# Runs of four chunks of V, eight score pairs between them, and one head's scores in a dense bank

## The chip, the cores and the metric

The kernel runs on one core of one Trainium2 chip. The metric is the device time of one execution in microseconds; before the change its median over three runs is 1396.16 us (1395.28 to 1396.99).

## The reference

One transformer block: layer norm, attention with 32 query heads of 16 dimensions and one shared key and value head, a residual, a second layer norm and a GEGLU feed-forward, all in float32 for 2048 tokens of 512 features.

```python
def _A_ref(x, wq, wk, wv, wo):
    q = (x @ wq).reshape(B, S, H, Dh)       # B, S, D, H = 1, 2048, 512, 32; heads ahead of tokens
    k = x @ wk
    v = x @ wv
    scores = jnp.einsum("bhqd,bkd->bhqk", q, k) * (Dh ** -0.5)
    p = _softmax(scores, axis=-1)
    o = jnp.einsum("bhqk,bkd->bhqd", p, v)
    return o.transpose(0, 2, 1, 3).reshape(B, S, H * Dh) @ wo
...
def _B_ref(x, w_gate, w_up, w_down):        # w_gate, w_up: 512 x 1792
    return (_gelu(x @ w_gate) * (x @ w_up)) @ w_down
...
h = x + _A_ref(_layernorm(x, axis=-1), A_wq, A_wk, A_wv, A_wo)
h2 = h + _B_ref(_layernorm(h, axis=-1), B_w_gate, B_w_up, B_w_down)
```

## The kernel before

The queries are taken in four blocks of 512 tokens (b). Attention goes through a block by eight groups of four heads (g), and through each group by sixteen chunks of 128 keys (kc), so there are 512 chunks in all. For a chunk, TensorE makes two **score pairs** (`scores`, L363). A pair is two heads that run side by side in the two row halves of the array, the contraction rows 0 to 63 and 64 to 127, and fills one buffer `s` of two PSUM banks. ScalarE turns each pair into weights with one exponential of 1024 columns (L374), which goes to half of the tile `p`. The chunk's **V matmuls** (`weigh`, L376) then multiply the four heads' weights by V, in four column tiles of 32, into `acc`. The profile counts each of these float32 matmuls twice, so a chunk is eight rows there. There are two `s` buffers, five `p` buffers (`PB`) and one `acc`.

The **dense work** of a block, its output projection (`pp`), gate, up and down products (`pg`, `pu`, `pd`), is done while attention goes through the next block. Each product is a sum of 9 to 18 terms with a contraction of 128. It is computed in two halves: `rows(0)` runs all terms with the contraction rows 0 to 63, `rows(1)` with rows 64 to 127, each into a bank of its own, and VectorE adds the two. A call of `step` (L837) issues one half step of each, the second one `LAG` = 6 steps behind, and the two run side by side in the array as the heads of a score pair do. Three PSUM banks (`spare`, d0 to d2) go round among the halves; a bank goes to the end of the list when its last matmul is issued, and whoever takes it next waits until it was read.

The order on TensorE, ScalarE and GpSimd is the one in which the code is written, and in the loop at L1167 that holds for SyncE and VectorE too. The loop goes through `CYCLES`. A woven cycle first finishes two or three pending chunks (`finish`, the V matmuls; `evacuate` after a group's last chunk) and then follows a string in which `s` is a score pair and `d` a dense step. Three cycles, with 3, 3 and 2 chunks, are one list: 8 chunks, 16 score pairs and 36 dense steps. Where too few steps are available, the second string is used, with a chunk (`v`) after every second pair and no dense work: a **pause**. Ahead of a cycle, `before` issues the tanh of finished gates (`bend`), the work that is left for VectorE (`later`), and the transpositions of the second layer norm's output (`turn`, L621), which take one of the three dense banks.

In the last block nothing is left to weave, and its dense work is the tail (`last_dense`) after the loop.

Of the kernel before, what the change touches and what calls it, by code (L numbers as in the profile page):

```python
# [9 lines left out]
F32 = mybir.dt.float32  # L10
# [9 lines left out]
P = 128  # L20
# [32 lines left out]
BOUND_LISTS = (3, 4)  # L53

HOLD = -4

# [3 lines left out]
def kernel(  # L60
# [97 lines left out]
    def run(outer, first):  # L158
# [204 lines left out]
        def scores(i, p, qg, kc, u):  # L363

            third = width == 1 and (2 * i + u) % 3 == 2
            pool, tag, bufs = (ps, "s3", 1) if third else (pss, "s", 2)
            s = pool.tile([P, 2, T], F32, tag=tag, bufs=bufs, name=f"s_{i}_{u}")
            for a in range(2):
                rows = slice(64 * a, 64 * a + KR)
                nc.tensor.matmul(  # L370
                    s[:, a, :], kaug[rows, kc * P : (kc + 1) * P], qg[rows, u, :],
                    start=True, stop=True,
                )
            nc.scalar.activation(p[:, 2 * u : 2 * u + 2, :], s, AF.Exp, scale=SCALE)  # L374

        def weigh(acc, p, kc):  # L376
            for j in range(4):
# [428 lines left out]
        built = []  # L806

        def rows(a):
            nonlocal at
            i = 0  # L810
            while i < len(queue):
                name, n, terms, done, ready = queue[i]
                i += 1
                if a == 0:
                    assert ready is None or ready()
                    left[0], at = n, i
                    built.append([])
                    source = iter(terms())
                sent = built[i - 1]
                tag, bank = take_bank(f"{name}_{a}")  # L820
                r = slice(64 * a, 64 * a + 64)
                for k in range(n):
                    if a == 0:
                        sent.append(next(source))
                        left[0] -= 1
                    lhsT, rhs, _ = sent[k]
                    nc.tensor.matmul(  # L827
                        bank, lhsT[r], rhs[r], start=(k == 0), stop=(k == n - 1),
                        skip_group_check=True,
                    )  # L830
                    if k == n - 1:
                        spare.append(tag)
                        done(a, bank)
                        side(2)
                    yield

        def step(first=True):  # L837
# [4 lines left out]
            if ahead > LAG or not first:  # L842
                assert ahead > 0
                next(seconds)
                ahead -= 1

# [197 lines left out]

        cur = {}

        def score(n):

            nonlocal acc
            i, u = divmod(n, 2)  # L1050
            b, r = divmod(i, PER)
            g, kc = divmod(r, KC)
            if u == 0:
                if kc == 0:
                    cur["qg"] = qgs.pop((b, g))
                    acc = psa.tile([P, T], F32, tag="acc", bufs=1, name=f"acc_{b}_{g}")
                if kc == 2 and b * NG + g + 1 < NB * NG:
                    key = divmod(b * NG + g + 1, NG)
                    qgs[key] = load_q(*key)
                cur["p"] = sb.tile([P, 4, T], F32, tag="p", bufs=PB, name=f"p_{i}")  # L1060
            scores(i, cur["p"], cur["qg"], kc, u)
# [11 lines left out]
        width = 1  # L1073


        n, lead = 0, 2 * PER + 23
        with tc.manual_schedule(engines={mybir.EngineType.SP, mybir.EngineType.DVE}):
            parts = None
            if first:
                work = later_q()  # L1080
                parts = part_weights(early.enter_context(tc.tile_pool(name="parts", bufs=1)))


            normed = True
# [12 lines left out]
            def norm():  # L1097
                nonlocal normed
                if not normed:
                    next(work)  # L1100
                    normed = True

            def pace():
                nonlocal n, parts, db, tiny
                if n == 2 * PER:
                    drain()
                    for _ in parts or ():
                        pass
# [12 lines left out]
                if n == 2 * PER + 8:  # L1121
                    prime()

            moves = {"s": pace, "p": visit, "n": norm, "v": partial(finish, 1)}
            for move in OPENING + PERIOD * (PER // KC):
                moves[move]()
            while n < lead:
                pace()
                if n % 4 == 2 and len(pend) > 2 and n < lead - 1:
                    finish(1)  # L1130
                elif n % 4 == 0:
                    finish(len(pend) - 2)
# [5 lines left out]
        def catch_up():  # L1138
            while ahead > 0:
                step(False)  # L1140
# [23 lines left out]
        fixed.enter_context(  # L1164
            tc.manual_schedule(engines={mybir.EngineType.SP, mybir.EngineType.DVE})
        )
        for i in range(-((lead - end) // 16)):  # L1167
            if first and i in BOUND_LISTS:
                bound_flag(BOUND_LISTS.index(i))
            for count, woven, plain in CYCLES:  # L1170
                idle = available() < woven.count("d")
                if idle:
                    while available():
                        step()
                    if at == len(queue) or queue[at][0].startswith("pg"):
                        catch_up()
                bent = before(idle)
                if n == end and not last_x:
                    prepare_x()
                if not idle:  # L1180
                    finish(count)
                for key in bent:
                    later.extend(gate(*key))
                for move in plain if idle else woven:
                    if move == "d":
                        step()
                    elif move == "v":
                        if n == end and not last_x:
                            prepare_x()
                        finish(1)  # L1190
                        clock += 4
                    elif n < end:
                        score(n)
                        n += 1
                        clock += 1
# [386 lines left out]
```

## Time and profile before

| what | value |
|---|---|
| median of three runs | 1396.16 us |
| the profiled execution: its own time / its span | 1397.61 us / 1395.8 us |
| granted TensorE clock | 1.000 |
| ScalarE's share of the span / VectorE's | 74% / 47% |
| loop with the woven dense work, about 304.8 to 1252.6 us | 947.8 us |
| tail after it | 143.2 us |
| number of V runs in the whole program, of 3, 2 and 1 chunks | 91, 86, 67 |

PE is TensorE, PEld its loads of weights, ACT ScalarE, DVE VectorE. A row of the timeline has the start, the length, the engine, the line of the program, what is written from what, the shape and, behind it, how long the engine sat idle before it and on whom it waited. Rows of one kind that follow each other are merged: the length is then that of all. The length of one matmul covers its way through the array, and matmuls overlap, so the distance between starts tells what one costs.

### The profile page before, as it was taken

Reading aid. Unit: us, or ns where it says so; the run is one execution under the profiler, and the core shown is the slowest. Engines: PE = TensorE matmul, PEld = TensorE weight load, DVE = VectorE, ACT = ScalarE, POOL = GpSimd, SP = SyncE. Lnnn points to the kernel's source line nnn. Section 1 sums busy time; section 2 is a strip of 40 time slices with the busy share of each in tenths; the row PEclk is TensorE's granted clock in tenths of the full one; section 3 lists DMA queues with packets and bytes.
Section 4 is the critical chain, followed back from the end, with each engine's and each line's share of the span. In section 5 each row is a group of like instructions: output and inputs, shape, how many; then the busy total and the mean of one; then the engine's idle time right before and its main releaser. Section 6 shows DMA issues by size and latency. Waiting matters only on the chain.

```text
span 1395.8 us, 25287 instructions
## 1 busy us (share of the span) xinstructions
PE 1379.5 (99%) x10406; PEld 753.3 (54%) x10406; DVE 651.0 (47%) x1097; ACT 1034.1 (74%) x1157; POOL 239.8 (17%) x346
## 2 busy tenths in 40 slices
PE   9999999999999999999999999999999999999998
PEld 7533333325555555545555555545555555558886
DVE  7413131314354444548364444448364453546665
ACT  8799999997787777877787777787778777772000
POOL 7576777621000000002000000001000000011000
PEclk9999999999999999999999999999999999999999
DMA  5565776753232333311522433321433333233552
GB/s 163 167 216 184 235 235 233 220 181 133 73 106 74 118 104 103 116 60 46 181 94 81 134 103 103 104 66 31 148 103 104 118 103 103 91 123 126 187 205 94
DMA packets 66783, 180.32 MB, mean 129 GB/s; under 512 B 9672, under 2 KB 9672, under 8 KB 66628
## 3 DMA queue, kind: packets, MB, share of 16 engines
q1 hardware_dynamic: 55324, 143.29, 31.0%
q0 software_dynamic: 10208, 35.26, 7.6%
q8 instruction: 84, 1.38, 0.4%
q14 instruction: 39, 0.32, 0.1%
q10 hardware_dynamic: 1128, 0.07, 0.1%
HBM read 130.87 MB, written 47.45 MB: 128 GB/s over the span
## 4 chain that ended last, share of the span: by engine, by line
PE 94%; ACT 2%; DMA 1%; DVE 1%; issue 1%; SPq 0%; POOL 0%; ACTq 0%; POOLq 0%
PE acc L378 33%; PE s L370 20%; PE pg L827 9%; PE pu L827 8%; PE pd L827 7%; PE pq L219 3%; PE pd L865 3%; PE pg L865 3%; PE pu L865 3%; PE pp L827 2%; ACT p L374 2%; PE pp L929 1%; PE pd_rest L877 1%; DMA x<-in_A_x_dram 1%; PE pk L1327 1%
## 5 line engine op out<-in xcount | busy, mean ns | idle before, releaser
L374 ACT ACTIVATE p<-s 128x1024 f32<-128x1024 f32 x1024 | 959.6, 1037 | 223.7 <-PE s L370 220.6
L378 PE MATMUL acc<-p,v_sb 128*32 128x512 f32 x4096 | 490.0, 598 | 0.0
L370 PE MATMUL s<-qg,kaug 50*128 50x512 f32 x1984 | 388.3, 426 | 4.2 <-ACT p L374 4.1
L370 PEld LDWEIGHTS s<-qg,kaug 50*128 50x128 f32 x1984 | 169.4, 184 | 281.7 <-ACT p L374 123.5
L378 PEld LDWEIGHTS acc<-p,v_sb 128*32 128x32 f32 x4096 | 108.7, 109 | 233.1 <-issue 218.7
L827 PE MATMUL pg<-x2h,w 64*128 64x512 f32 x672 | 175.2, 392 | 0.0
L827 PE MATMUL pu<-x2h,w 64*128 64x512 f32 x672 | 174.5, 392 | 0.0
L827 PE MATMUL pd<-w,gh 64*128 64x512 f32 x624 | 124.7, 394 | 1.9 <-DVE h L615 1.6
L757 DVE TENSOR_TENSOR h<-h,pd 128x512 f32<-128x512 f32 x80 | 55.0, 687 | 140.7 <-PE pd L827 140.6
L137 POOL TENSOR_SCALAR rstd<-mv 128x1 f32<-128x1 f32 x16 | 3.6, 223 | 649.1 <-DVE mv L135 648.8
L827 PEld LDWEIGHTS pg<-x2h,w 64*128 64x128 f32 x672 | 95.5, 186 | 11.4
L827 PEld LDWEIGHTS pu<-x2h,w 64*128 64x128 f32 x672 | 95.7, 186 | 10.8
L827 PE MATMUL pg<-x2l,w 64*128 64x512 f32 x336 | 99.9, 392 | 0.0
L827 PE MATMUL pu<-x2l,w 64*128 64x512 f32 x336 | 99.9, 391 | 0.0
L827 PEld LDWEIGHTS pd<-w,gh 64*128 64x128 f32 x624 | 69.7, 185 | 15.0 <-DVE h L615 2.5
L391 DVE COPY oT<-acc 128x512 f32<-128x512 f32 x32 | 22.1, 692 | 112.5 <-PE acc L378 112.3
L983 ACT ACTIVATE ga<-ga 128x512 f32<-128x512 f32 x14 | 8.8, 632 | 88.5 <-DVE ga L980 88.5
L827 PE MATMUL pd<-w,gl 64*128 64x512 f32 x312 | 72.1, 392 | 0.0
L694 DVE TENSOR_TENSOR g<-g,pg 128x512 f32<-128x512 f32 x42 | 28.8, 685 | 90.8 <-PE pg L827 90.8
L414 DVE RECIPROCAL oc<-oc 128x128 f32<-128x128 f32 x64 | 56.7, 923 | 21.4 <-DMA oc<-acc_d 17.6
L690 DVE COPY g<-pg 128x512 f32<-128x512 f32 x42 | 29.1, 692 | 72.0 <-PE pg L827 72.0
L694 DVE TENSOR_TENSOR u<-u,pu 128x512 f32<-128x512 f32 x42 | 28.8, 686 | 68.6 <-PE pu L827 68.6
(255 smaller groups left out, 1493.1 us busy)
## 6 DMA issues: line engine op xcount, KB each, us to landing
w<-w_d SPq DMA_DIRECT2D x126, 512.0 KB
w<-w_d SPq DMA_DIRECT2D x21, 1024.0 KB
qg<-q_d SPq DMA_DIRECT2D x62, 200.0 KB
q_d<-qh SPq DMA_DIRECT2D x32, 256.0 KB
acc_d<-oT SPq DMA_DIRECT2D x31, 256.0 KB
oc<-acc_d SPq DMA_DIRECT2D x124, 64.0 KB
w_d<-w_0b POOLq DMA_DIRECT2D x14, 512.0 KB, 4.6
w_d<-w_1b POOLq DMA_DIRECT2D x14, 512.0 KB, 3.4
```

What stands on the lines that cost most here:

```text
L219: nc.tensor.matmul(pq, wt[c][:, d, :], xt[:, d, :], start=(n == 0), stop=(n == 3 * DC - 1),)
L370: nc.tensor.matmul(s[:, a, :], kaug[rows, kc * P : (kc + 1) * P], qg[rows, u, :], start=True, stop=True,)
L374: nc.scalar.activation(p[:, 2 * u : 2 * u + 2, :], s, AF.Exp, scale=SCALE)
L378: nc.tensor.matmul(acc[32 * j : 32 * j + 32, :], v_sb[:, kc, :], p[:, j, :], start=(kc == 0), stop=(kc == KC - 1), skip_group_check=True,)
L391: nc.vector.tensor_copy(oT, acc)
L414: nc.vector.reciprocal(oc[:, 1, sl], oc[:, 1, sl])
L690: nc.vector.tensor_copy(half, bank)
L694: nc.vector.tensor_tensor(half, half, bank, op=ALU.add)
L757: nc.vector.tensor_tensor(hs[b, t], hs[b, t], bank, op=ALU.add)
L827: nc.tensor.matmul(bank, lhsT[r], rhs[r], start=(k == 0), stop=(k == n - 1), skip_group_check=True,)
L865: nc.tensor.matmul(bank, lhsT, rhs, start=(i == 0), stop=(i == len(ts) - 1))
L877: nc.tensor.matmul(bank, lhsT, rhs, start=(i == 0), stop=(i == len(ts) - 1))
```

## The change

The lead, in which attention runs without dense work, ends one score pair later, with four chunks pending. From there on every cycle finishes four chunks (`RUN`) in one run. A woven cycle has eight score pairs and 18 dense steps. Where a dense bank is free (its last use at least `EMPTY` = 6 counts ago), the cycle ends with one head of a ninth pair: its scores go into that dense bank (`score_half`, a = 1, beside a half step of `rows(0)`), with an exponential of 512 columns. The pair's other head comes first after the V run (a = 0, beside a half step of `rows(1)`), in half of an `s` buffer and with an exponential of its own. The next cycle then has seven whole pairs (`WOVEN`) instead of eight (`FRESH`). Pauses are of one chunk each, and the rules for when to pause, catch up and turn are new.

```diff
-CYCLES = (
-    (3, "ssdddddsdddsddds", "vssvssvs"),
-    (3, "ssdddddsdddsddds", "vssvssvs"),
-    (2, "ssdddddsdddsdddsddds", "ssvssvss"),
-)
+RUN = 4
+WOVEN = "sdddsdddsdddsdddsdddsdds"
+FRESH = "ssdddddsdddsdddsdddsddsds"
+PAUSE = "ssvssvssvss"
+EMPTY = 6
+AHEAD = {240: 3, 248: 2}
...
+        def score_half(n, a):
+            if a == 1:
+                cur["open"] = open_pair(n)
+            i, u, b, g, kc = cur["open"]
+            assert u == 0
+            if a == 1:
+                tag, s = take_bank(f"s_{i}_{u}_1")
+                spare.append(tag)
+            else:
+                s = pss.tile([P, 2, T], F32, tag="s", bufs=2, name=f"s_{i}_{u}_0")[:, 0, :]
+            score_head(s, cur["qg"], kc, u, a)
+            nc.scalar.activation(cur["p"][:, 2 * u + a, :], s, AF.Exp, scale=SCALE)
...
-        n, lead = 0, 2 * PER + 23
+        n, lead = 0, 2 * PER + 24
...
-        for i in range(-((lead - end) // 16)):
-            if first and i in BOUND_LISTS:
-                bound_flag(BOUND_LISTS.index(i))
-            for count, woven, plain in CYCLES:
-                idle = available() < woven.count("d")
-                if idle:
-                    while available():
...
+        odd, cycle = False, 0
+        while pend:
...
+            last = n >= end - 2 * RUN
+            steps = WOVEN.count("d") + 1
+            want = 12 if urgent() else steps * AHEAD.get(n % (2 * PER), 1)
+            idle = n == end or available() < (want if n < end - 2 * PER // 8 else steps)
...
+            bent = before(idle)
...
+            behind = idle and n < end and turns_left()
+            idle = idle and not behind and available() < want
+            finish(1 if idle else RUN)
+            clock += 4 if idle else 4 * RUN
+            if behind:
+                for b_t in list(scaled_at):
+                    del scaled_at[b_t]
+                    turn(*b_t)
...
+            if idle:
+                moves = "2" * odd + PAUSE[odd:]
+            else:
+                part = not last and not scaled_at
+                moves = ("2" + WOVEN if odd else FRESH) + "d1"[part]
+            for move in moves:
+                if move == "d":
+                    if available():
+                        step()
...
+                elif move == "1":
+                    if clock - freed.get(spare[0], -EMPTY) < EMPTY or not available():
+                        if available():
+                            step()
+                        odd = False
+                    else:
+                        score_half(n, 1)
+                        step(second=False)
+                        odd = True
+                elif move == "2":
+                    score_half(n, 0)
+                    if ahead > LAG:
+                        step(first=False)
+                    n, odd = n + 1, False
```

In the rows below, `s_i_u` are the scores of chunk i's pair u (a third number is the single head), `p_i` the weights of chunk i, `acc` the sums over V, `pg`, `pu`, `pp` and `pd` the halves of dense products, and `pxt` a transposition.

The first place is on TensorE in block 1, where the first gate and up products run. Before, a V run and what stands around it:

```order
L370 MATMUL s_157_1_3837<-qg_1_1_3236,kaug_70 128x512 x2
L378 MATMUL acc_1_1_3502<-p_155_3784,v_sb_71 32x512 x4
L378 MATMUL acc_1_1_3502<-p_156_3805,v_sb_71 32x512 x4
L378 MATMUL acc_1_1_3502<-p_157_3826,v_sb_71 32x512 x4
L370 MATMUL s_158_0_3854<-qg_1_1_3236,kaug_70 128x512 x2
L370 MATMUL s_158_1_3858<-qg_1_1_3236,kaug_70 128x512 x2
```

Now, on the same engine, one chunk earlier in the same group:

```order
L380 MATMUL s_155_1_3826<-qg_1_1_3236,kaug_70 128x512 x2
L380 MATMUL s_156_0_1_3831<-qg_1_1_3236,kaug_70 128x512
L836 MATMUL pu_0_0_0_3806<-x2h_0_3257,w1_0_0_1_3265 128x512
L386 MATMUL acc_1_1_3474<-p_152_3761,v_sb_71 32x512 x4
L386 MATMUL acc_1_1_3474<-p_153_3776,v_sb_71 32x512 x4
L386 MATMUL acc_1_1_3474<-p_154_3797,v_sb_71 32x512 x4
L386 MATMUL acc_1_1_3474<-p_155_3819,v_sb_71 32x512 x4
L380 MATMUL s_156_0_0_3851<-qg_1_1_3236,kaug_70 128x512
L836 MATMUL pg_0_0_1_3783<-x2h_0_3257,w1_0_0_0_3261 128x512
L380 MATMUL s_156_1_3861<-qg_1_1_3236,kaug_70 128x512 x2
```

Four chunks stand in a row, and pair 0 of chunk 156 is cut in two: one head ahead of the run and one behind it, each beside one half step of dense work.

The second place is on TensorE where the first of block 0's four token tiles is transposed. Before:

```order
L370 MATMUL s_147_0_3593<-qg_1_1_3236,kaug_70 128x512 x2
L628 MATMUL pxt_0_0_3597<-ident_60,xb_0_0_3259 128x128 x4
L378 MATMUL acc_1_1_3502<-p_144_3503,v_sb_71 32x512 x4
L378 MATMUL acc_1_1_3502<-p_145_3528,v_sb_71 32x512 x4
L378 MATMUL acc_1_1_3502<-p_146_3568,v_sb_71 32x512 x4
```

And now, on the same engine:

```order
L380 MATMUL s_147_1_3595<-qg_1_1_3236,kaug_70 128x512 x2
L380 MATMUL s_148_0_1_3600<-qg_1_1_3236,kaug_70 128x512
L836 MATMUL pp_0_2_0_3545<-wo_hi_72,o_lo_0_1712 128x512
L636 MATMUL pxt_0_0_3606<-ident_60,xb_0_0_3259 128x128 x4
L386 MATMUL acc_1_1_3474<-p_144_3475,v_sb_71 32x512 x4
L386 MATMUL acc_1_1_3474<-p_145_3528,v_sb_71 32x512 x4
L386 MATMUL acc_1_1_3474<-p_146_3555,v_sb_71 32x512 x4
L386 MATMUL acc_1_1_3474<-p_147_3586,v_sb_71 32x512 x4
```

The transposition takes the bank that the single head `s_148_0_1` took two instructions earlier, since that bank is the first in the list.

The third place is on TensorE at the last of these transpositions, of which the first gate product needs all four. Before, three runs of one chunk stand between `pxt_0_2` and `pxt_0_3`, and two runs of one chunk and one of three between `pxt_0_3` and `pg_0_0_0`. Now:

```order
L836 MATMUL pp_0_3_1_3671<-wo_hi_72,o_lo_0_1712 128x512
L636 MATMUL pxt_0_1_3718<-ident_60,xb_0_1_3263 128x128 x4
L636 MATMUL pxt_0_2_3727<-ident_60,xb_0_2_3267 128x128 x4
L386 MATMUL acc_1_1_3474<-p_148_3599,v_sb_71 32x512 x4
L386 MATMUL acc_1_1_3474<-p_149_3646,v_sb_71 32x512 x4
L386 MATMUL acc_1_1_3474<-p_150_3677,v_sb_71 32x512 x4
L386 MATMUL acc_1_1_3474<-p_151_3694,v_sb_71 32x512 x4
L636 MATMUL pxt_0_3_3752<-ident_60,xb_0_3_3613 128x128 x4
L380 MATMUL s_152_0_3762<-qg_1_1_3236,kaug_70 128x512 x2
L380 MATMUL s_152_1_3766<-qg_1_1_3236,kaug_70 128x512 x2
L836 MATMUL pg_0_0_0_3770<-x2h_0_3257,w1_0_0_0_3261 128x512
```

The pauses are gone there, and two score pairs are all that stands between the last transposition and the first matmul that reads its copy.

In the whole program the V runs go from 244 to 197 (90 of four chunks, one of five, 41 of two, 65 of one). In the loop there are 79 cycles that have both a head behind the run and one ahead of the next, two of them with transpositions, eight cycles with eight whole pairs that begin without one, five of them full woven ones, and 12 pause runs of one chunk where there were 13. 84 score pairs are cut in two. The number of score, V and dense matmuls is the same. At the end of block 0's gates VectorE's order changes too: its add of the product `pd_0_8_1`'s second half now stands ahead of the two instructions that make `gh` and `gl` of the last gate (f = 13); before, it stood behind them.

More of the change, by code (lines that the diff above doesn't have):

```diff
@@ L368, in scores, with score_head @@
             for a in range(2):
[L369 to L374, printed above, removed]
+                score_head(s[:, a, :], qg, kc, u, a)
+            nc.scalar.activation(p[:, 2 * u : 2 * u + 2, :], s, AF.Exp, scale=SCALE)
+        def score_head(s, qg, kc, u, a):
+            rows = slice(64 * a, 64 * a + KR)
+            nc.tensor.matmul(
+                s, kaug[rows, kc * P : (kc + 1) * P], qg[rows, u, :], start=True, stop=True
+            )
         def weigh(acc, p, kc):
@@ L806, in run @@
         built = []
+        freed = {}
         def rows(a):
@@ L832, in rows @@
                         spare.append(tag)
+                        freed[tag] = clock
                         done(a, bank)
@@ L835, in rows, with step @@
                     yield
-        def step(first=True):
+        def step(first=True, second=True):
             nonlocal ahead, clock
@@ L841, in step @@
                 ahead += 1
-            if ahead > LAG or not first:
-                assert ahead > 0
+            if second and ahead > (LAG if first else 0):
                 next(seconds)
@@ L1045, in run, with open_pair @@
         cur = {}
-        def score(n):
+        def open_pair(n):
             nonlocal acc
@@ L1060, in score @@
                 cur["p"] = sb.tile([P, 4, T], F32, tag="p", bufs=PB, name=f"p_{i}")
+            return i, u, b, g, kc
+        def score(n):
+            i, u, b, g, kc = open_pair(n)
             scores(i, cur["p"], cur["qg"], kc, u)
@@ L1128, in run @@
                 pace()
-                if n % 4 == 2 and len(pend) > 2 and n < lead - 1:
+                if n > lead - 6:
+                    finish(len(pend) - RUN)
+                elif n % 4 == 2 and len(pend) > 2:
                     finish(1)
@@ L1166, in run, with urgent @@
         )
-        for i in range(-((lead - end) // 16)):
-            if first and i in BOUND_LISTS:
-                bound_flag(BOUND_LISTS.index(i))
-            for count, woven, plain in CYCLES:
-                idle = available() < woven.count("d")
-                if idle:
-                    while available():
-                        step()
[L1175 to L1195, printed above, removed]
+        def urgent():
+            i = at - 1 if left[0] else at
+            return i < len(queue) and queue[i][0].startswith("pp") and any(
+                queue[j][0].startswith("pg") for j in range(i, min(i + TB + 1, len(queue)))
+            )
@@ new lines, in turns_left @@
+        def turns_left():
+            return scaled_at and all(
+                turned.get(b, 0) + sum(b == other for other, _ in scaled_at) == TB
+                for b, _ in scaled_at
+            )
+        odd, cycle = False, 0
+        while pend:
+            if first and cycle in BOUND_CYCLES:
+                bound_flag(BOUND_CYCLES.index(cycle))
+            cycle += 1
+            last = n >= end - 2 * RUN
+            steps = WOVEN.count("d") + 1
+            want = 12 if urgent() else steps * AHEAD.get(n % (2 * PER), 1)
+            idle = n == end or available() < (want if n < end - 2 * PER // 8 else steps)
+            if idle and (n == end or urgent()):
+                while available():
+                    step()
+            if idle and not available() and (
+                at == len(queue) or queue[at - 1][0].startswith("pp")
+            ):
+                catch_up()
+            bent = before(idle)
+            if last and not last_x:
+                prepare_x()
+            behind = idle and n < end and turns_left()
[6 more added lines that the diff above has]
+                    turn(*b_t)
+            for key in bent:
+                later.extend(gate(*key))
+            side(2 * len(bent))
+            if idle:
[6 more added lines that the diff above has]
+                    if available():
+                        step()
+                elif move == "v":
+                    finish(1)
+                    clock += 4
+                elif move == "1":
[12 more added lines that the diff above has]
+                    n, odd = n + 1, False
+                elif n < end:
+                    score(n)
+                    n += 1
+                    clock += 1
@@ L1196, in run @@
+        assert not odd
+        while available():
+            step()
         fixed.close()
```

2 lines of the change are left out of this document (1 added, 1 removed).

## The prediction, made before the run

> **What bounds the kernel now.** I read the page's busy times first, then its chain, its groups, and last the loop and one list of three cycles by windows (columns: length, PE, PEld, DVE, ACT and POOL busy with instructions, granted clock, DMA share, GB/s).
>
> ```profile
> PE 1379.5 (99%) x10406; PEld 753.3 (54%) x10406; DVE 651.0 (47%) x1097; ACT 1034.1 (74%) x1157; POOL 239.8 (17%) x346
> PE 94%; ACT 2%; DMA 1%; DVE 1%; issue 1%; SPq 0%; POOL 0%; ACTq 0%; POOLq 0%
> L374 ACT ACTIVATE p<-s 128x1024 f32<-128x1024 f32 x1024 | 959.6, 1037 | 223.7 <-PE s L370 220.6
> ...
> 304.80:1252.60 947.80, 943.17 (x7788) 513.36 (x7788) 468.83 (x795) 729.76 (x799) 23.83 (x41) 1.00 0.31 103
> 700.75:720.86 20.11, 20.11 (x171) 11.14 (x169) 13.69 (x22) 16.01 (x19) 0.00 (x0) 1.00 0.25 83
> ```
>
> TensorE bounds the whole: 99% busy, 94% of the chain. But inside a cycle ScalarE is close behind. A list of eight chunks takes 20.11 us, so **10.055 us for four chunks**, and ScalarE idles in it only 4.1 us, and mostly while V runs. The timeline of that list, DVE and dense rows left out, shows it:
>
> ```profile
> 700.75 2.78 PE L378 MATMUL acc<-p,v_sb 128*32 128x512 f32 x24
> 703.46 0.73 PE L370 MATMUL s<-qg,kaug 50*128 50x512 f32 x4
> 704.06 4.69 ACT L374 ACTIVATE p<-s 128x1024 f32<-128x1024 f32 x5 [1.53 <-PE s L370]
> 705.14 0.18 PEld L370 LDWEIGHTS s<-qg,kaug 50*128 50x128 f32 x2 [0.22 <-ACT p L374]
> 705.48 0.40 PE L827 MATMUL pu<-x2h,w 64*128 64x512 f32 x1
> 707.45 1.92 PE L378 MATMUL acc<-p,v_sb 128*32 128x512 f32 x16
> 709.31 0.73 PE L370 MATMUL s<-qg,kaug 50*128 50x512 f32 x4
> 709.85 5.61 ACT L374 ACTIVATE p<-s 128x1024 f32<-128x1024 f32 x6 [1.10 <-PE s L370]
> 709.88 0.40 PE L827 MATMUL pu<-x2h,w 64*128 64x512 f32 x2
> 713.86 0.40 PE L370 MATMUL s<-qg,kaug 50*128 50x512 f32 x2
> 714.19 2.78 PE L378 MATMUL acc<-p,v_sb 128*32 128x512 f32 x24
> ```
>
> Distances between starts give the constants. A run of three chunks takes 703.46 − 700.75 = 2.71, one of two 709.31 − 707.45 = 1.86: a chunk is 0.85, and **0.16** is paid for each run. The third cycle (20 slots, a slot being a score pair or a dense step) takes 714.19 − 709.31 = 4.88. Its first two slots take 709.88 − 709.31 = 0.57 and its last 714.19 − 713.86 = 0.33. With a slot of **0.2335** in between, the first two are 0.11 too long and the last 0.10. So one change from the rest to V and back costs 0.16 + 0.11 + 0.10 = **0.37 us**.
>
> On ScalarE the first exponential starts 709.85 − 709.31 = 0.54 behind the first score, six follow each other at (5.61 − 1.037) / 5 = **0.913**, and one takes 1.037. With two `s` buffers, a pair waits for the exponential two pairs earlier: 704.06 + 1.037 = 705.10, the weight load comes 0.04 later at 705.14, and the dense step behind it at 705.48, one slot behind 705.25. So a waiting pair's slot begins **0.15** behind the end of that exponential.
>
> **The change, part by part.** The work on TensorE is the same; 244 − 197 = 47 V runs go. If nothing came late in their place, that would be 47 × 0.37 = 17.4 us. [...]
>
> What comes late is ScalarE. A single head needs an exponential of 512 columns, which before doesn't have. Rows of such shapes bound it:
>
> ```profile
> L125 ACT ACTIVATE o_hi<-oc 128x128 fp32r<-128x128 f32 x4 | 1.2, 312 | 8.0 <-DVE oc L431 8.0
> L125 ACT ACTIVATE qh<-pq 128x512 fp32r<-128x512 f32 x2 | 1.2, 598 | 1.3 <-PE pq L219 1.3
> 1273.83 2.08 ACT L965 ACTIVATE hp<-pp 128x512 f32<-128x512 f32 x4
> L965 ACT ACTIVATE hp<-pp 128x512 f32<-128x512 f32 x4 | 2.1, 624 | 0.0
> ```
>
> Four copies of that shape out of PSUM follow each other at (2.08 − 0.62) / 3 = 0.49. The other way: 384 columns more cost L125 598 − 312 = 286 ns, so 512 fewer take 0.38 off an exponential, and its pitch becomes 0.913 − 0.38 = 0.53 and its length 0.66. I take **0.51**. Two halves then cost 1.02 where a whole one costs 0.913.
>
> *Term 1, the woven cycle.* V takes 2.71 + 0.85 = 3.56. Behind it the half `2` and pair 1 start; the exponentials follow each other from 0.54 on. Pair 7 is slot 24: it could start at 0.11 + 24 × 0.2335 = 5.71. It waits for the fifth whole exponential, which ends at 0.54 + 0.51 + 4 × 0.913 + 1.037 = 5.74, and its slot begins at 5.89: a **wait of 0.18**. Then come its slot, slot `1` and the last 0.10: 5.89 + 0.47 + 0.10 = 6.46, and the cycle is 3.56 + 6.46 = 10.02 against 10.055. Over 79 such cycles: −0.035 × 79 = **−2.8 us**. The exponentials of pair 7 and of `1` lie beside V, as does the tanh of a gate, so that no V matmul waits.
>
> The ends: without a wait the cycle is 3.56 + 0.11 + 26 × 0.2335 + 0.10 = 9.84, which is −17.0 us; with a pitch of 0.62, the whole length of such a copy, it is 10.13, +5.9 us.
>
> [...]
>
> *Term 2, cycles with eight whole pairs.* Five full ones begin without a half. Pair 8, also slot 24, waits for the sixth exponential: 0.54 + 5 × 0.913 + 1.037 + 0.15 = 6.29; with the same ending 6.29 + 0.57 + 3.56 = 10.42, +0.365 each, **+1.8 us**.
>
> *Term 3.* One pause fewer. The two V runs below stand 349.72 − 347.85 = 1.87 apart, while a chunk's own work is 0.85 + 2 × 0.2335 = 1.32; somewhat less than the difference goes: **−0.4 us**.
>
> *Term 4, waits where a block begins.* Rows from the first of them:
>
> ```profile
> 339.43 1.36 PE L628 MATMUL pxt<-ident,xb 128*128 128x128 f32 x8
> 340.72 1.06 PE L378 MATMUL acc<-p,v_sb 128*32 128x512 f32 x8
> 342.81 0.55 DVE L604 TENSOR_SCALAR xb<-h,mv,rstd 128x512 f32<-128x512 f32 x1 [0.99 <-POOL rstd L138]
> 345.31 0.69 DVE L634 TENSOR_TENSOR x2l<-pxt,x2h 128x512 fp32r<-128x512 f32 x1
> 346.17 0.66 PE L628 MATMUL pxt<-ident,xb 128*128 128x128 f32 x4
> 346.75 0.50 PE L370 MATMUL s<-qg,kaug 50*128 50x512 f32 x2
> 347.58 0.69 DVE L634 TENSOR_TENSOR x2l<-pxt,x2h 128x512 fp32r<-128x512 f32 x1
> 347.85 1.07 PE L378 MATMUL acc<-p,v_sb 128*32 128x512 f32 x8
> 349.72 1.06 PE L378 MATMUL acc<-p,v_sb 128*32 128x512 f32 x8
> 650.73 0.18 PEld L827 LDWEIGHTS pd<-w,gh 64*128 64x128 f32 x1 [1.23 <-DVE h L615]
> 972.25 0.50 PE L827 MATMUL pd<-w,gh 64*128 64x512 f32 x1 [0.81 <-DVE h L615]
> L757 DVE TENSOR_TENSOR h<-h,pd 128x512 f32<-128x512 f32 x80 | 55.0, 687 | 140.7 <-PE pd L827 140.6
> L724 DVE CAST gh<-ga 128x512 fp32r<-128x512 f32 x42 | 17.5, 418 | 0.3
> ```
>
> - `pxt_0_0` takes the bank of `s_148_0_1`, and now must wait for that head's exponential. In the cycle of term 1 this starts behind seven whole ones, at 0.54 + 0.51 + 7 × 0.913 = 7.44, ends about 8.08 and frees TensorE at 8.23, where the transposition could start at 6.36: **+1.9**. Everything on TensorE queues behind it, the V run first.
> - `pg_0_0_0` now stands right behind `pxt_0_3`. In the old order the last copy of tile 2 ends at 345.31 + 0.69 = 346.00, 6.57 behind the start of `pxt_0_1` at 339.43. Now the V run begins 1.29 behind that start (340.72) and `pxt_0_3` at 4.85; with 0.58 for it (346.75 − 346.17) and 0.57 for two pairs, `pg_0_0_0` is due at 6.0. VectorE makes tile 3's `x2h` and `x2l` only from 6.57 on, to 7.95, and the second half step, due at 6.2, needs both: **+1.9** with the 0.15. The runs of one chunk hid this before.
> - Gate 13 of block 0: `gh` is now made behind the add of `pd_0_8_1`. Its last matmul's 0.39, some 0.1 to release, 0.69 for the add and 0.42 for the cast make 1.6, less the slot in between: **+1.4** on the next half step that reads `gh`.
> - At block 1, TensorE waits 1.23 for a bank that VectorE's add L615 frees. In the new order the same wait stands at block 1 but no longer at block 2, where TensorE stood idle 0.81 at 972.25 (its weights, as at block 1, somewhat longer): **−1.2**.
>
> Each wait lets ScalarE catch up, which spares the next cycle's 0.18 three times: −0.5. Term 4 is **+3.5**, with ends of 0 (VectorE and ScalarE are there in time) and +8 (each wait is met in all three blocks).
>
> **The sum** is −2.8 + 1.8 − 0.4 + 3.5 = **+2.1 us** against the profiled execution, 1397.61, which was itself 1.45 above the median of 1396.16; the rest of the span is not touched. On the median that is 1398.2. A gain of some tenths at the lead's end and the catch-up at the end of the loop, where 41 runs of two are about what they were, is not counted; I take half a microsecond off for it: **1397.6 us**, no change that can be told. About 0.2% (2.8 us) is what a measurement of this kernel can tell from none.
>
> **The rivals.**
> - *The switches saved come in full or nearly.* Pair 7 doesn't wait, or half as long: the fifth exponential would have to end 0.18 earlier. For it: half an exponential may be ready to start earlier than 0.54, since one head fills it, and pitch 0.49 already takes 0.02 off. Against it: 0.913 and 1.037 stand 1024 times in the profile. Half the wait is −7.1 us, 1390.5; none is −14.2, **1383.4**.
> - *Slower: the half exponentials become ScalarE's bound.* If a half costs close to its whole length, each 0.01 us of pitch is 0.79 us over 79 cycles. From a pitch of about 0.53 on the sum is over 0.2% slower; at 0.53, the L125 estimate, 1399.2; at 0.62 **1406.3**. For it: the wait of 705.14 shows that ScalarE sets the pace already. Against it: L965's 0.49.
> - *The change doesn't do what it says.* A half head is given up where its bank isn't free. The order of instructions shows 84 pairs cut and 90 runs of four; this is excluded.
>
> **How the numbers follow.** No change that can be told 0.38; faster 0.35, with most of it between 1386 and 1393; slower 0.27, between 1399 and 1406. The terms alone lean to slower, but the slower case needs every one of term 4's waits in full, and the faster one only a tenth of a microsecond in each cycle. The likeliest case's own range is 1393.4 to 1399.0; with the others, 1386 to 1405 leaves out about 2 in 10.
>
> **What would show it.** In the profile after: cycles of 10.02 (against 9.84 for the first rival, 10.13 for the second); a weight load of the last whole pair that waits 0.1 to 0.3 for ACT; half exponentials of about 0.64 that follow at 0.51; and once, where block 0's tiles are transposed, 1.9 of idle time at `pxt` that ends with an exponential and 1.9 at the first `pg` that ends with VectorE. What would make it wrong: a start of the half's exponential well before 0.54, a slot longer than 0.2335 where a half score stands beside a dense half step, or a V run of four whose last chunk waits for the seventh exponential.

## The result, and the profile after

The changed kernel takes **1406.63 us** (median of four runs, 1405.21 to 1408.69) against 1395.72 us for the kernel before, measured beside it: a ratio of 1.0078, 95% interval 1.006 to 1.0095. That is 11 us slower, outside the predicted range of 1386 to 1405. The profiled execution took 1408.69 us, 11.1 more than the one of before. One execution reported below, of the twelve of the last version measured, ran at a granted clock of 0.593 and took 2249 us; the ratio of that version leaves it out.

From the page, the busy times, the chain and two groups:

```profile
PE 1383.1 (98%) x10406; PEld 758.4 (54%) x10406; DVE 657.5 (47%) x1097; ACT 1035.2 (74%) x1241; POOL 239.5 (17%) x346
PE 89%; ACT 5%; DVE 3%; DMA 2%; issue 1%; POOL 0%; SPq 0%; ACTq 0%; POOLq 0%
...
L376 ACT ACTIVATE p<-s 128x1024 f32<-128x1024 f32 x940 | 878.5, 1050 | 40.7 <-PE s L380 37.9
L1089 ACT ACTIVATE p<-s 128x512 f32<-128x512 f32 x168 | 106.0, 631 | 190.7 <-PE s L380 150.8
```

And the loop by windows, with the columns of the prediction:

```profile
304.80:1263.60 958.80, 945.75 (x7784) 517.64 (x7786) 473.73 (x795) 731.24 (x884) 23.77 (x41) 1.00 0.31 101
```

The loop is 11 us longer at practically the same number of matmul rows (7784, before 7788), and TensorE has lost some of its share of the chain, most of it to ScalarE (2% before, 5% now) and VectorE (1%, now 3%). ScalarE's own sum hardly grew: 168 half exponentials took the place of 84 whole ones.

A woven cycle in the timeline, dense rows left out:

```profile
707.67 3.64 PE L386 MATMUL acc<-p,v_sb 128*32 128x512 f32 x32
711.24 0.50 PE L380 MATMUL s<-qg,kaug 50*128 50x512 f32 x1
711.78 0.60 ACT L1089 ACTIVATE p<-s 128x512 f32<-128x512 f32 x1 [2.00 <-PE s L380]
712.27 6.52 ACT L376 ACTIVATE p<-s 128x1024 f32<-128x1024 f32 x7
717.01 0.19 PEld L380 LDWEIGHTS s<-qg,kaug 50*128 50x128 f32 x2 [0.30 <-ACT p L376]
717.36 0.39 PE L380 MATMUL s<-qg,kaug 50*128 50x512 f32 x1
717.68 1.07 PE L386 MATMUL acc<-p,v_sb 128*32 128x512 f32 x8
```

V takes 711.24 − 707.67 = 3.57, the half exponential starts 0.54 behind the first score, the whole ones follow 712.27 − 711.78 = 0.49 later, and the last whole pair's weights wait 0.30 for ScalarE. Not all of the 0.30 is lost: the dense step ahead of this pair starts at 716.75 and the one behind it at 717.36, which is 0.14 more than two slots. The cycle is 717.68 − 707.67 = **10.01** against the predicted 10.02. That is also the median of the 79; eleven are longer, by 0.13 to 2.5 (the longest, at 323.93, ends with the first transposition and its wait). So the regular cycle does what was forecast, and the loss lies elsewhere.

**Where.** Count the work that TensorE has done by its matmuls of V, scores and dense steps, at the durations of the prediction, and compare when each of the two traces has done as much. The difference is the lag, in us. The lag of the changed kernel is −0.2 us at 290 us. It grows by 3.2 by 320 us, by 2.8 more by 370, falls by 0.5 up to 590, grows by 5.0 by 695 and 0.9 by 919, by 0.8 by 1000, and falls by 0.9 to the end: 11.1 us. The pauses have moved, too: of the kernel before, five stand at 341 to 350 us, where now there is none, three at 613 to 617 (now four at 593 to 599) and five at 931 to 939 (now eight at 919 to 933). So from 320 to 370 us the saved pauses hide a part of what the waits and the clock cost there. The waits of TensorE in the whole program name the places:

```profile
PE s L380 <- ACT p L376: 7.3, 23, 0.7
PE s L380 <- DVE h L626: 1.8, 2, 1.2
PE pxt L636 <- ACT p L1089: 1.7, 1, 1.7
...
PE pd L836 <- DVE gh L732: 1.1, 1, 1.1
PE pd L836 <- DVE x2l L642: 0.7, 1, 0.7
PE pg L836 <- DVE g L702: 0.7, 4, 0.2
PE pg L836 <- DVE x2h L641: 0.7, 1, 0.7
```

(us in total, times, longest.) In the trace of before ScalarE is waited for less, and the add L615, which is L626 now, in two waits of 1.6 in all:

```profile
PE s L370 <- ACT p L374: 4.1, 12, 0.7
```

Two more things stand in no list of waits. At the lead's end, and again behind the first gate product, the granted clock of before was 1.00 and now is 0.83 over 10 us (310 to 320 and 350 to 360; first the two rows of before, then the two of now):

```profile
310.00:320.00 10.00, 10.00 (x80) 4.65 (x80) 0.94 (x2) 7.16 (x8) 0.00 (x0) 1.00 1.03 411
350.00:360.00 10.00, 9.84 (x78) 4.41 (x74) 0.00 (x0) 7.89 (x9) 0.00 (x0) 1.00 0.01 2
310.00:320.00 10.00, 9.58 (x64) 3.86 (x64) 1.51 (x3) 5.56 (x7) 0.00 (x0) 0.83 1.03 408
350.00:360.00 10.00, 9.10 (x60) 5.37 (x53) 4.41 (x7) 4.10 (x5) 0.97 (x2) 0.83 0.21 65
```

In the records of the clock these are two stretches of 3.41 us at 0.50, from 310.92 and from 355.29. And the lead's last six pairs run without any V, at ScalarE's pace, before a run of five chunks:

```profile
306.38 0.91 PE L380 MATMUL s<-qg,kaug 50*128 50x512 f32 x4
307.71 0.50 PE L380 MATMUL s<-qg,kaug 50*128 50x512 f32 x2 [0.42 <-ACT p L376]
...
310.46 0.50 PE L380 MATMUL s<-qg,kaug 50*128 50x512 f32 x2 [0.42 <-ACT p L376]
310.89 6.18 PE L386 MATMUL acc<-p,v_sb 128*32 128x512 f32 x40
317.00 0.74 PE L380 MATMUL s<-qg,kaug 50*128 50x512 f32 x4
```

### The profile page after: what moved, and what is told of

Read it like the earlier page. It is cut to its first block, busy times and chain, and to the rows that moved or that the text cites. A ratio compares the mean times of both kernels' runs of the same rounds, so it can differ in the third digit from the quotient of the medians.

```text
span 1406.9 us, 25386 instructions
## 1 busy us (share of the span) xinstructions
PE 1383.1 (98%) x10406; PEld 758.4 (54%) x10406; DVE 657.5 (47%) x1097; ACT 1035.2 (74%) x1241; POOL 239.5 (17%) x346
## 4 chain that ended last, share of the span: by engine, by line
PE 89%; ACT 5%; DVE 3%; DMA 2%; issue 1%; POOL 0%; SPq 0%; ACTq 0%; POOLq 0%
PE acc L386 32%; PE s L380 19%; PE pg L836 8%; PE pu L836 8%; PE pd L836 7%; ACT p L376 5%; PE pq L225 3%; PE pd L874 3%; PE pg L874 3%; PE pu L874 3%; PE pp L836 1%; PE pp L938 1%; DMA w<-w_d 1%; DMA x<-in_A_x_dram 1%; DVE xt L657 1%
## 5 line engine op out<-in xcount | busy, mean ns | idle before, releaser
L376 ACT ACTIVATE p<-s 128x1024 f32<-128x1024 f32 x940 | 878.5, 1050 | 40.7 <-PE s L380 37.9
L386 PE MATMUL acc<-p,v_sb 128*32 128x512 f32 x4096 | 481.9, 599 | 0.0
L380 PE MATMUL s<-qg,kaug 50*128 50x512 f32 x1984 | 421.5, 426 | 9.2 <-ACT p L376 7.3
L380 PEld LDWEIGHTS s<-qg,kaug 50*128 50x128 f32 x1984 | 184.7, 184 | 272.4 <-ACT p L376 141.3
L386 PEld LDWEIGHTS acc<-p,v_sb 128*32 128x32 f32 x4096 | 113.1, 109 | 253.2 <-issue 241.4
L1089 ACT ACTIVATE p<-s 128x512 f32<-128x512 f32 x168 | 106.0, 631 | 190.7 <-PE s L380 150.8
L836 PE MATMUL pg<-x2h,w 64*128 64x512 f32 x672 | 209.7, 401 | 1.4 <-DVE g L702 0.7
L836 PE MATMUL pu<-x2h,w 64*128 64x512 f32 x672 | 208.4, 398 | 0.4 <-DMA w<-w_d 0.4
L836 PE MATMUL pd<-w,gh 64*128 64x512 f32 x624 | 115.5, 394 | 1.9 <-DVE gh L732 1.1
L836 PE MATMUL pd<-w,gl 64*128 64x512 f32 x312 | 81.1, 400 | 0.0
L702 DVE TENSOR_TENSOR u<-u,pu 128x512 f32<-128x512 f32 x42 | 28.8, 685 | 85.2 <-PE pu L836 56.4
L702 DVE TENSOR_TENSOR g<-g,pg 128x512 f32<-128x512 f32 x42 | 28.8, 687 | 67.7 <-PE pg L836 52.2
```

What stands on the lines that cost most here:

```text
L380: nc.tensor.matmul(s, kaug[rows, kc * P : (kc + 1) * P], qg[rows, u, :], start=True, stop=True)
L386: nc.tensor.matmul(acc[32 * j : 32 * j + 32, :], v_sb[:, kc, :], p[:, j, :], start=(kc == 0), stop=(kc == KC - 1), skip_group_check=True,)
L702: nc.vector.tensor_tensor(half, half, bank, op=ALU.add)
L836: nc.tensor.matmul(bank, lhsT[r], rhs[r], start=(k == 0), stop=(k == n - 1), skip_group_check=True,)
L1089: nc.scalar.activation(cur["p"][:, 2 * u + a, :], s, AF.Exp, scale=SCALE)
```

## The experiments

Theory A: the woven cycles save their switches but give most of it back in the wait of the last pair, and the 11 us are lost where the lead ends and where blocks begin. Its rivals are named with each run. The kernel before ran beside each: its median was 1395.72 us beside the first four, 1396.44 beside the next two and 1397.42 beside the last two.

### The last pair behind the single head

```diff
-                moves = ("2" + WOVEN if odd else FRESH) + "d1"[part]
+                moves = "2" + WOVEN if odd else FRESH
+                moves = moves[:-1] + "1s" if part else moves + "d"
```

The rest of the edit is bookkeeping: the open chunk's second pair is scored behind the next chunk's first head.

> The changed kernel with the last two slots of a cycle exchanged: the single head goes first, the last whole pair behind it (slot 25 instead of 24). Nothing else moves. Theory A (the switches are saved, but the last whole pair waits 0.15 to 0.18 us for ScalarE in every woven cycle; the rest of the loss lies where blocks begin): slot 25 is due at 0.11 + 25 x 0.2335 = 5.95, later than the exponential's 5.89, so the wait goes, the cycle falls from 10.006 to about 9.85, 79 x 0.155 = 12 us and some more in the cycles with eight pairs: about 1393 us. Theory B (the single heads and their exponentials cost the time themselves): the cycle stays at 10.0, 1405 to 1407 us.

Measured: 1398.71 us, 7.9 less; 1.0022 of before, interval 1.0012 to 1.0032. The timeline of a cycle's end:

```profile
398.24 0.18 PEld L380 LDWEIGHTS s<-qg,kaug 50*128 50x128 f32 x1
398.51 0.19 PEld L380 LDWEIGHTS s<-qg,kaug 50*128 50x128 f32 x2
399.07 0.64 PE L386 MATMUL acc<-p,v_sb 128*32 128x512 f32 x4
399.22 0.64 ACT L1089 ACTIVATE p<-s 128x512 f32<-128x512 f32 x1
```

The last pair's weights (398.51) don't wait any more, and the median cycle is 9.88 instead of 10.01. Per cycle that is 0.12, not the 0.155 expected, and four cycles with late adds (see the gate's run below) take 10.63 instead of 10.39 and give back 1 us: hence 8 us and not 12. Theory A holds for the cycle: the wait was real, and it had eaten two thirds of the 0.19 that one V run fewer in eight chunks saves in each cycle (0.37 / 2).

### Without single heads

```diff
-                part = not last and not scaled_at
+                part = False
```

> The changed kernel without any single head: every cycle has four chunks, eight whole pairs and 18 dense steps. Theory A: pair 8 in slot 24 waits for the sixth whole exponential, as in the cycles of 10.39 and more that begin without a half, so a cycle takes 10.39 to 10.43, 79 x 0.4 = 32 us more, less the 1.7 at the first transposition: 1435 to 1440 us. Theory B: without the single heads' cost a cycle is at 10.0 or below, 1395 to 1406 us.

Measured: one run of 1448.59 us. The timeline shows pair 8 waiting for the sixth exponential:

```profile
428.22 0.73 PE L380 MATMUL s<-qg,kaug 50*128 50x512 f32 x4
428.82 7.44 ACT L376 ACTIVATE p<-s 128x1024 f32<-128x1024 f32 x8 [2.54 <-PE s L380]
434.48 0.18 PEld L380 LDWEIGHTS s<-qg,kaug 50*128 50x128 f32 x2 [0.61 <-ACT p L376]
435.13 3.64 PE L386 MATMUL acc<-p,v_sb 128*32 128x512 f32 x32
```

A cycle takes 10.49 (median of 83), 0.06 to 0.1 more than expected, and one cycle at 644 us takes 16.7, with a granted clock of 0.50 from 655.06 to 661.89 (0.97 over 600 to 700 us). These two account for the time above the 1435 to 1440 us expected. So the single heads don't cost the time, they save 38 us of waiting (79 × 0.48); without them runs of four are 53 us slower than the kernel before. Theory B falls.

### The lead's end

```diff
-                if n > lead - 6:
+                if n > lead - 2:
```

> The changed kernel, with the lead's end built up later: the last four pairs run without V instead of the last six, so one V chunk more lies beside ScalarE's work, the run of five becomes one chunk and a later run of three. Theory A (3.2 us are lost at the lead's end, where TensorE idles and its clock is halved for some 3.5 us behind that): 0.9 us less if the clock still halves, up to 3 us less if it doesn't, 1403.5 to 1405.8 us. Theory B (what is lost there would be lost later anyway): no change, 1406.6 us.

Measured: 1406.53 us, no change that can be told. The trace does show the gain at its place: the run is now three chunks and takes 314.18 − 310.89 = 3.29 (more than the 2.71 of the prediction, since weight loads at 312.28 and 313.20 wait for ScalarE), and the first dense step starts at 314.75 instead of 317.57. The lag is 2.8 us less than the changed kernel's from there on, and 3.1 at the end.

```profile
310.89 3.37 PE L386 MATMUL acc<-p,v_sb 128*32 128x512 f32 x24
314.18 0.73 PE L380 MATMUL s<-qg,kaug 50*128 50x512 f32 x4
```

But the profile it is compared with is the slowest of the changed kernel's four runs. These were 1405.21 and 1405.74 at a mean clock of 0.999, and 1407.52 and 1408.69 at 0.996; the four of this edit had 1405.56 (0.998) to 1407.42 (0.996). The clock's variation between executions is as large as the gain, and the times alone leave open whether it is 0 or 1 us. An estimate from the traces: this one has one stretch of 3.41 us at half the clock behind the lead (1.00 over 310 to 320 us, 0.83 over 350 to 360), the changed kernel's has two. One such stretch costs up to half of its 3.41, which is 1.7 us, so at least some 1.4 of the 3.1 us come from the order.

### The first transposition's bank

```diff
-                    if clock - freed.get(spare[0], -EMPTY) < EMPTY or not available():
+                    if scaled_at or clock - freed.get(spare[0], -EMPTY) < EMPTY or not available():
```

> The changed kernel, but no single head in a cycle's end while a transposition stands ready, so that the first transposition doesn't take a bank that waits for an exponential. Four single heads fewer. Theory A: the wait of 1.7 us at the first transposition goes, and the cycle behind it, with eight whole pairs, takes 0.4 more: 1.3 us less, 1405.3 us, if the order behind it stays as it was. Theory B (the wait moves on to the first gate product, which needs all four tiles, of which the last is late anyway): no change, 1406.6 us.

Measured: 1406.88 us, no change in the times. In the trace the transposition doesn't wait any more, but the first gate product does as before:

```profile
334.19 0.63 PE L636 MATMUL pxt<-ident,xb 128*128 128x128 f32 x4
...
350.97 0.66 PE L636 MATMUL pxt<-ident,xb 128*128 128x128 f32 x4
352.96 0.50 PE L836 MATMUL pg<-x2h,w 64*128 64x512 f32 x1 [0.68 <-DVE x2h L641]
353.69 0.50 PE L836 MATMUL pg<-x2l,w 64*128 64x512 f32 x1 [0.23 <-DVE x2l L642]
```

The lag falls by 1.7 at the transposition, 0.4 come back by 370 us, and 1.0 more is won at the next block. This trace has a second use. Its lead's end has the very instructions of the changed kernel, but its clock stayed at 1.00 there:

```profile
312.60 4.50 PE L386 MATMUL acc<-p,v_sb 128*32 128x512 f32 x40
317.03 0.73 PE L380 MATMUL s<-qg,kaug 50*128 50x512 f32 x4
```

The run of five takes 4.43 here and 6.11 in the changed kernel's profile. The granted clock was 0.72 over the 6.11, and 6.11 × 0.72 = 4.40, so the **1.7 us** between them is the clock alone, and it isn't lost at this place in every execution. Here the half clock came earlier, from 286.27 to 289.68, where the two kernels' orders are still the same, and the lag is 1.5 us already at 290: the chunk of V that starts at 305.39 in the changed kernel's trace starts 1.71 later, at 307.10.

### The gate ahead of the copy of acc

In the changed kernel's timeline, VectorE at the end of a group's last V run, with the half exponential and the matmul behind it:

```profile
694.64 0.69 DVE L698 COPY g<-pg 128x512 f32<-128x512 f32 x1 [1.18 <-PE pg L836]
700.99 0.69 DVE L399 COPY oT<-acc 128x512 f32<-128x512 f32 x1 [5.66 <-PE acc L386]
701.38 0.60 ACT L1089 ACTIVATE p<-s 128x512 f32<-128x512 f32 x1 [1.92 <-PE pg L836]
701.60 0.68 DVE L720 SCALAR_TENSOR_TENSOR ga<-ga,g 128x512 f32<-128x512 f32 x1
702.92 0.68 DVE L702 TENSOR_TENSOR g<-g,pg 128x512 f32<-128x512 f32 x1
703.66 0.49 PE L836 MATMUL pg<-x2h,w 64*128 64x512 f32 x1 [0.18 <-DVE g L702]
```

The copy stands first in VectorE's order and waits 5.66 us for V. The gate, whose tanh is done at 699.46, and the add that frees a bank queue behind it, and TensorE's next start, at 703.66, comes 0.58 behind the last one, 0.35 late.

```diff
+            for key in bent:
+                later.extend(gate(*key))
+            side(4 * len(bent))
             finish(1 if idle else RUN)
...
-            for key in bent:
-                later.extend(gate(*key))
-            side(2 * len(bent))
```

> The changed kernel with one thing moved on VectorE: the four instructions that finish a gate stand ahead of the copy of acc after a group's last chunk, not behind it. In the changed kernel this copy waits for the end of the V run of four (idle 5.66 us behind 695.33), and four cycles of block 2 and 3 take 10.39 because the add that frees a bank (L702) stands behind it; at 616.88 TensorE waits 1.28 for gh behind the same copy. Theory A (VectorE's order of issue at the V run is what costs there): 4 x 0.38 + 1.28 = 2.8 us less, 1403.8 us, and no cycle of 10.39 with an idle time that ends with L702. Theory C (these banks are late for another reason, such as the single head that takes one of them): the cycles stay at 10.39, 1406.6 us.

Measured: 1406.36 us, again no change that can be told from the times. In the trace:

```profile
698.89 0.69 DVE L720 SCALAR_TENSOR_TENSOR ga<-ga,g 128x512 f32<-128x512 f32 x1 [3.73 <-ACT ga L714]
...
700.79 0.60 ACT L1089 ACTIVATE p<-s 128x512 f32<-128x512 f32 x1 [1.94 <-PE pg L836]
...
701.41 0.69 DVE L399 COPY oT<-acc 128x512 f32<-128x512 f32 x1
702.01 0.68 DVE L702 TENSOR_TENSOR g<-g,pg 128x512 f32<-128x512 f32 x1
```

The add now starts 702.01 − 700.79 = 1.22 behind the half exponential's start, instead of 1.54, and TensorE's waits for L702 and for gh are gone. The lag falls by 1.31 at 616 us and by about 0.25 at each of the four cycles. With a shorter DMA wait at 694 that is 2.7 in all, near the 2.8 expected. So Theory A holds in the trace. The clock can hide it in the times: this profile's mean was 0.995, with three stretches at half the clock instead of two (0.98 over 200 to 290 us, 0.83 over 310 to 320, 0.85 over 350 to 360), and its lag was 1.2 us larger already ahead of the loop.

### The four edits together

> The changed kernel with the four edits together: last pair behind the single head, later build-up at the lead's end, no single head while a transposition stands ready, gate ahead of the copy of acc. Theory A: from the 1398.7 us of the exchanged slots, 4 x 0.75 + 1.3 for the gates (the cycles with the late add take 10.63 there), about 2 for the transposition and 1 for the lead: about 1391.5 us, 0.3% faster than the kernel before. If the waits only move on: 1396 to 1399 us, no faster than before.

Measured: **1392.45 us** (seven runs), 0.9976 of the kernel before, interval 0.9962 to 0.999: a version that beats both, by 14 and 4 us. The chain and the busy times of its page:

```profile
PE 1371.3 (99%) x10406; PEld 764.2 (55%) x10406; DVE 658.5 (47%) x1097; ACT 1034.7 (74%) x1239; POOL 240.5 (17%) x346
PE 93%; ACT 3%; DVE 2%; issue 1%; POOL 0%; DMA 0%; SPq 0%; POOLq 0%; ACTq 0%; DVEq 0%
```

TensorE's share of the chain is back to 93%, from 89%. The other three edits, which singly showed nothing in the times, thus take some 6 us more than the exchange of slots alone (1.0022 to 0.9976, intervals apart); how that divides among the three, the times don't show. The two waits for the add L626 are still there, 2.3 us in all, and no run here tests them. Against the trace of before, this one is level at 338 us, 3.0 ahead at 576, level again behind the pauses at 641 and 6.9 ahead at 1242: the cycles gain, and the places where a block begins give part of it back.

### Pauses ahead of the first gate product

The first of these two runs has this edit alone, the second has it with the four edits.

```diff
-            behind = idle and n < end and turns_left()
+            behind = False
```

> The changed kernel without the rule that runs a block's last transpositions behind a V run of four and goes straight on with the first gate product: pauses of one chunk come there again, as in the kernel before. Theory A (pg_0_0_0 is late because nothing stands between it and the last transposition): the waits of 0.83 and 0.49 at 353 to 355 us go, the pauses cost some 0.45 each, and up to 1 us is won there in the profile: about 1405.5 us at the clock of the first profile. Theory B (the pauses cost what the waits cost): the same place is passed no earlier.

> The four edits of the best version, and no rule for the last transpositions either. Theory A: up to 1 us less than 1392.5 for each of the blocks where it applies: 1390 to 1392 us. Theory B: 1392 to 1394 us.

Measured: 1407.9 us (one run), and with the four edits 1394.51, 0.998 of before (0.997 to 0.9991), no better than 0.9976, and half a microsecond above what Theory B expected. In the trace of the first, `pg_0_0_0` no longer waits, but four pauses stand there, and the lag falls by only 0.3, although the clock stayed at 1.00 there, and the cycles behind that place lose some 1.4 again. This speaks for Theory B: the wait costs about what the pauses cost that hid it before, and is then no loss against the kernel before. It rests on one trace, in which a new wait for `gh` (2.22 us at 948.69) adds to the time elsewhere.

## Why the prediction was wrong

The steps that failed are those of the places between regular cycles. The lead's end was put at half a microsecond of gain and cost 3.2 us. A wait for a bank, put at −1.2, did not go: 2.5 us of such waits stand where there were 1.6. And the adds behind the copy of acc (1.4 us), two pairs at ScalarE's pace (1.2) and the half clock were no terms at all. One by one:

- **The woven cycle (term 1) was right**: 10.01 for 10.02, the half exponentials' pitch 0.49 (the lower of the two rows), and a wait for ScalarE in the last pair, which the exchange of two slots took away. That wait, 0.30 at 717.01, went with ScalarE's work unchanged (763.1 us busy from 290 to 1395 us in the changed kernel, 763.6 with the slots exchanged), so it came from the order and not from ScalarE's pace as a whole.
- **Cycles with eight pairs (term 2)**: 10.50 for 10.42, nearly right. The fifth of them, at 611.26, takes 11.80 with the wait for `gh`.
- **Three waits of term 4 were there**: `pxt_0_0` 1.7 for 1.9; `pg_0_0_0` 0.67 and 0.23 and the times around them, 1.3 for 1.9; `gh` 1.28 for 1.4 (the distance of starts, less a slot), for which the copy of acc ahead of the gate is a cause as well, since the wait went when the gate was moved ahead of it.
- **The fourth part of term 4 failed.** "At block 1, TensorE waits 1.23 for a bank … no longer at block 2: −1.2." No such wait went. There are three, and other instructions take the bank: 1.24 and 0.55 for the add L626, each at a single head, and 0.74 for `x2l` at a dense step. I had read only whether the old wait stays, not who takes the bank next.
- **The lead's end was dismissed** as "a gain of some tenths". It is the largest single miss: 3.2 us in the profiled execution, some 1.5 for six pairs at ScalarE's pace with no V beside them, and 1.7 for the clock behind them. The 1.7 depend on the execution, as the transposition's run shows.
- **Not in the sum at all**: the adds behind the copy of acc, four times 0.35 and a share of the gh wait; two pairs at ScalarE's pace at 344 us (waits of 0.39 and 0.41); and the lower clock behind `pg_0_0_0`, some 1.5.

The forecast stood at +1.6 us against the profiled execution, and it was +11.1. Of these 9.5 us the lead's end is 3.7 with the half microsecond that was taken off for it, the adds 1.4, the pairs at 344 us 1.2 (0.77 and 0.91 between starts, less two slots), the clock behind the gate product 1.5, and the banks 2.1 (2.5 of waits where there were 1.6, instead of 1.2 less): 9.9. The woven cycles (1.1 better than forecast) and the three waits (0.9 less) take 2.0 off. Some 8 of the 9.5 us are accounted for, the rest isn't assigned. These are sizes read from the trace; the runs above test the lead's end, the adds and the first transposition, but not the banks and not the pairs at 344 us.

The second rival's price, 1406.3, is met by luck, for its mechanism isn't there: the half exponentials cost what L965 said.

What stays open: how much of the 11 us is the clock in a run without profile. The changed kernel's two runs at 0.999 were 1405.2 and 1405.7, the two at 0.996 some 2.6 us longer. If the first two had no half clock in the loop, which can't be shown without a trace of them, the clock is some 2.6 of 12.4 us in the slower two and nothing in the others. Between the two profiles, two stretches of 3.41 us at half cost at most 3.4 of the 11.1.

## What to carry to other kernels

A change of a loop's rhythm is summed for the regular cycle first, but its risk lies at the seams: list every place where the old order had slack (a pause, a build-up, a copy at the end of a run) and price it with the new run length, on every engine whose order is fixed. Where a longer run on one engine is awaited by an instruction at the head of another engine's queue, move what doesn't need the run ahead of it. When a saving disappears, exchange the last waiting step with one that needn't wait: here that alone was worth 8 us.

## What the hardware showed that was not expected

TensorE's granted clock fell to half for 3.41 us behind stretches in which it stood partly idle (a slot of 0.2335 every 0.91 us from 307 to 310.5). By the profile TensorE was busy for 1.96 us of the 3.41 ahead of the changed kernel's first stretch and for 2.51 ahead of its second. The V matmuls at 310.89 to 314.30 us follow each other at 0.85, and at 0.43 from there on, and the window of 312 to 314 us has a granted clock of 0.50.

It did so in some executions and not in others with the same instructions there. Over 310 to 320 us the granted clock was 0.83 in the traces of the changed kernel, of the exchanged slots, without single heads, with the gate moved, and with the pauses ahead of the first gate product alone. In that of the first transposition's run it was 1.00, though the same four pairs run ahead of V with the same idle times, 0.41 to 0.42 each, and the run of five took 4.43 us instead of 6.11. So the idle times alone don't settle it. In the three traces with the later build-up, where TensorE was busy for 10.00 of the 10 us from 300 and again of the 10 from 310, it was 1.00.

In the changed kernel's trace the clock is first full 7.13 us behind the start of the span, and its two stretches begin 303.79 and 348.16 us behind that, 89 and 102 times 3.413. In the trace of before it is first full at 5.30 us. Why one execution has such a stretch and another has none is not shown by these runs.
